# Turning the query weights on TensorE instead of by DMA, one slab fewer with normalized queries, and a new instruction order, in a four-layer attention and GLU kernel

## The chip, the cores and the metric

The kernel runs on one core of one Trainium2 chip. The metric is the device time of one execution in microseconds (us), and a kernel's time is the median of several executions. The core has five engines with an instruction queue each: TensorE (PE) for matrix products, VectorE (DVE), ScalarE (ACT), GpSimd (POOL) and SyncE (SP). SP here only issues DMA transfers, a transposing kind among them. Each engine executes its queue in order and waits on semaphores for the others.

## The reference

Four layers in a row act on x of 2048 positions by 512 channels, all in bf16: linear attention, GLU, linear attention, GLU. The weights are the same for both attentions and for both GLUs.

```
x = x + attention(layernorm(x));  x = x + glu(layernorm(x));  # twice

attention: q, k, v = x @ wqkv            # 32 heads of 16
  pq, pk = q @ w_phi, k @ w_phi          # per head, 16x16
  phi_q = [softmax(pq), softmax(-pq)];   phi_k likewise   # 32 features
  kv = phi_k^T v;   z = sum over positions of phi_k
  o = (phi_q kv) / (phi_q . z + 1e-6);   return o @ wo
glu: return (relu(x @ W_gate) * (x @ W_up)) @ W_down      # 1376 wide
```

## The kernel before

**Recording and order.** The kernel doesn't write its instruction streams out by hand. `build_kernel` records some 2100 operations with `op(...)`: an engine, a function that emits the instructions, the resources that it reads and writes, and an estimated cost. `schedule` then sorts them by a list scheduler with one priority for each operation, unpacked from the string `RANKS`; `MOVED` lists the operations (by number) which take their second engine (`alt`), mostly DVE in place of ACT or POOL and the other way round. `prepare` gives every operation the semaphore waits that its data and its buffers need. So `RANKS` and `MOVED` set the order on each engine, which engine some copies and small products use, and which of the buffers each tile takes. Once built, the order is fixed.

**Layers and tiles.** Layers are numbered 0 (attention), 1 (GLU), 2 (attention), 3 (GLU). A tile t is 128 positions (16 tiles), a slab s four tiles. The names used below are those of the operations, with the layer first: K0.4 is the key product of layer 0, tile 4.

**Start.** SP loads x in pieces, the key weights, the query weights (`wqn`, L561, one transfer into a part of the `Wd` buffer) and the value weights; POOL loads tiles 8 to 15 of x (L567) once tile 7 has landed. Forty small products (L571) warm PE up. The per-head matrix w_phi is multiplied into the weights: for that, the key weights are turned on PE (`turn`, L587: four 128x128 transposes per piece of 128 rows, "WkT") and copied out of PSUM by ACT and DVE (L477, L478). The products with the block-diagonal BD (L606) give Wkp and Wqp. The query weights are turned by four DMA transposes instead (L595, "WqT", flag `WQ_DMA`).

**Layer norm** (`ln`): statistics on DVE (L620, L621), ln and exp on ACT for the reciprocal root (L629, L631), y on DVE (L646) or POOL (L645). y is turned to yT by a DMA transpose (L660), or, for the tiles in `PE_Y`, on PE (L655) with a copy.

**Keys and values** (`kv_tile`, `features`): K (four matmuls of 512 columns, L682, for the first tile L686), two exps on ACT with signs +1 and -1 (L695), the sum over each head's 16 features (L703 on DVE, or a half sum on POOL, L700, and the rest on DVE, L701, for tiles in `POOL_Z`), the reciprocal as ln and exp on ACT (L717, L718) or on DVE (L720), and the norm, a product in place on DVE (L708). V is four matmuls (L739) and a copy. `kv_sums` then adds up keys times values over the tiles on PE (L786, "kv") and masks the sums into `kvs` on DVE (L809, L812) and, if any slab of the layer has normalized queries, also into `kvn` (L796, L799).

**Queries, two forms.** For a slab in the set `NQ`, `q_tile` makes normalized queries tile by tile just as keys are made, and two DMA transposes turn them (L767, "qT"). `attn_tile_n` then needs 8 products of 68 columns ("Rn", L901), a reciprocal on ACT (L906, L908) and two products on DVE (L913). For any other slab, `q_chunk` makes the exps already turned, without a sum: four times four matmuls of 512 columns (L754) and two exps each (L758). `attn_tile` then has 8 products of 144 columns ("R", L837) whose extra columns hold the sums, copies of them (L851), a chain of small operations for both signs' coefficients (p L858, den L860, ln and exp L862 and L863, coefficient L864), three products t on DVE (L874, L879) and their sum o (L883 on DVE, L884 on POOL). `finish_tile` turns o by DMA (L931) or on PE (L926), multiplies with wo (L936) and adds to x (L939).

**GLU**: gate and up products (L966), relu on ACT (L973), product on DVE (L974), a remainder of 96 columns ("rem", L994), and the down product ("d", L1020, L1022) with the sum into x on DVE (L1028).

The GLU weights are loaded by SP (L1052 to L1058) in the order of its queue; between them stand DMA transposes.

Of the kernel before, what the change touches and what calls it, by code (L numbers as in the profile page):

```python
# [421 lines left out]
def build_kernel(nc, A_x, A_wqkv, A_w_phi, A_wo, B_x, B_W_gate, B_W_up, B_W_down, out):  # L422
# [169 lines left out]
    if ("sp", "wqn") in LOADS or ("pool", "wqn") in LOADS:  # L592
        if WQ_DMA:
            for ic in range(4):
                op("sp", lambda e, ic=ic: e.dma_start_transpose(t_wq.ap()[:, :, ic * 128:(ic + 1) * 128], wqn[:, ic, :]), reads=[c_wqn, c_wd], writes=[c_wqT[ic]], dma="tr", nbytes=500, name="WqT",  # L595
                   after=chain["sp"][-1:])
# [511 lines left out]
ROUNDS = 8  # L1108

RANKS = (  # L1110
    '#{oD9YzH6+4hSI#fCnB3k_Q(E0SLqg`3C|BoCoIzT>ujZIS7FVEeH$<1OyETMF$)R%LhURjRvs?(g61d^aSe%b_W9pD+pTvjt5x>Y5-pb^#>;i=m+!%rT`ZJ',
# [3 lines left out]
    ')&|E0y#@^j<Ok{p2nRX_K?j`&AO_9`p$E_h)CbcC76`Qm;scEVp9kFsRs_8O%m)bp7zpD7+XSfwxd1>1BnRLJHV94!$p>-=7zaEDG6-o0jR$Q7oCb^r?gwrK',
    'l?7x6GzfkNBL`##wFa^W+XoK@76ASSY6c?++6SixpausA90zO#ng#I(x(4G0)(27s83>yOIR;7xl?F!!1P6)+mIliOOa^NPbOyx*L<Z6Y3J6sP+XmML@&!o-',
    'd<LEe$_D%e_y$)7DhH$n>;}XJMFs{2g9d#DR|l{MR0hNawg!U*8V4r^0|!|KXa|)C_Xha}Vg>F6F$O6Hdj^RHr3Oa_Ne7Dtg$D))IR}dep#}s7dIwzx$Om8r',
    'tOgMW_6L9kR0kIZbq7`lD+ZqgO9wCpEe09|6b3s6SO=;G<p**FxCS!@I0yU&@dbJY$^|F}>jYp1uLiXRng?G6JqGj!kp|cVNCtuj_5|4le+F9xss--`aR$By',
    'ItN1qE(bvc1qYi2Jq2+Ej|DIYvj><3vId3*-3E3B83uj@#s;1S;0A04F9uBpga<tb>;)(XP6o6GT?VKJzy|FGc?V(#6a_{FV+GO#st39U%LG~nr3EMi<_Aj!',
    'umwK_a0Y$`IRrxnHU{Vg`voBd<p#b5AP4USumlGM;s#{~(gREb(gxoHv<8?5g#)(-qzCi^Dg{aePz4?Z!vfj`#|6O!Km~6HZU*rNzz1pti3Pm{(*{ik%?BO_',  # L1120
    '?FY#Qfd#t-`UQ^!A_h7Ilm-6=X9l1Ls|QR6(*;=tiU-OBmj_b>y9a&*PzLk`X9dOu`2_+8*awCO^9C{o*anmbm;^Nit^<$<cLVkYD+lribp<2_j0ckhF$dQN',
    '!UyjM1O);Ft_DK~jRXk?a0HqLO$9Lp`Ul(x!v@C(3<uc;t_6GtGY6^z%?1AjH3nA%Ed=5PYX_MJUj()X(FSn`-38tTcn8r3@CQ%?9R}<J5C`Z6`v>3!hy~CF',
    'HU+c=8wP6y+y;{e;RLw{Mh89wf(2~`k_KV~69?Z00SAW$Ee9+IAqKMrHwHcivIUL>iv{ci9|tuDxCd_rTL&Qr*90X72L{vyLI-FB$Ob0|cm`(#DF=cE`vwID',
    'RRz`s$OJYA76&p1&IMHleFt0z69(-AX$Fl290unFUIpm|qXj+(od!P!@CJwn{smD5+yrI^tprO3QwE0x9tKJVI0n=MyalHPx&?OzF9qTRVFMlnIR)ee_XH3G',
    '4h0Yes|HgAXa)-gCI?{$TLzZ}&;=<4<^`q(vjh?bP6fmSs0HB#W(02qbq4PQp9V4n=md8K4FzNcWdv;ptOX7Rhz6nsQUtFA3j{a?MFoTfPX`PIfCdu<Wd%D0',
    'NCk@oBn9;a3I<9A2nPBD!UQJ;as~qh`~<-S>IJ6+ECyr*$OX0qQU(15odpmE<pr7qoC696_ysZrzXVSOqywo1umd^-Ed`7OHwCQ)vjZdqXa#u%GX%Q?tOO|p',
    '*98s-^Z|+jkOg-H^#sBN`2(K?N(09P$pn@JXafxdxB}S(X$98;`vaT=xdIvjzyi<%;{p=|vj8Fmu?3k0S_Ci!_yl?d@C0rI5(Mi8r~`Wh7zIQHX#}(cnF4_W',
    'F9bCN76Neu*aZRwOaxQ~vj&z0#scsIRRk^ufd&W#i3i{Wy#($AI|QHvE(JUUgaj)C5d{DQE(34}Nd-^`s|5@OBL<NL!3W|8S_bk45eS3^e+PpE6$t$XMFf}z',
    '_y<M?A_sj0_XWcT(g({14F=BzxCJW(zXgv56bCd1-UVU?y9Nsfd<7i`&jvIF76x1f+XX-dJO*I~2?Y-aRtBgBPX-kS0S0adSO)$B0R<lh$pxGRECp}{-2|cr',
    ')ds-^3I(G9qXvux5(TvcCI)#1wF43db_MDNqXVl1zXtOJw*zzppanh!)CRc*B?X=Z-~(X<%mr5ilmcA@MFTbi+XKi0wgTh>Yy+VLr30e`qy^go&jO<YqykX_',  # L1130
    'GX?zw0|wIrNC%JvyaW*j>jf191_ed~B?RXKas;&kD+E&mg#~y6wga02l>|crg#>W|o&x3rS_NAKSp<{=)dL#>-2<lrrUOm_=mO0I&I5A>AOoKR@&ZW%;{cii',
    'lmuG>69P~HI|C~MyaUbz%>&p1I{^s-!~&fIfdUr=F9YiW+5=DmR0GQckOEZ$-~vbjVF6DAAp!^i`2i0CJO!}?T?GpTBL%<(GzNbK)C7|SAO+e4a|F=@w*?~v',
    '{{$ul-UQ<XAq1}l7zTR<nFL$~76rHi4+R+o<OBc%h6C~hbOp=?`U7<Yp#}H?V+7L#=>(wzK?J!4sRR)O)dJiDxdW*I%mVxZC<Sx}{sbHaL<6P*$^x1KSOpvc',
    'V*}O#j05Qdzyuou#RCrmZ2|BFG6VVn2m>_&jRRl<hyxV_r2_Z><pYrf`2-dLg9E$*1_Vh2R|4V!djc*5QUi+ugaIA{`U2MhF$7Bls02p^bpp`?8w4-|9|SW4',
    '5(8QS0|Z_JKLf4;#sKF8e*_-|8wI)qrUjb>@dQ8w%mjx6hy-c`#stv?fdmN#>I60d;{??OHv{Yfh6G~<Rs$3S?gI}5h6UOIqy*&zq691i-UFfo^#QpA7z8u~',
    'Hw2XfjswpGDg$i-)&#5rz613GECa0vPy<*4B?mYIs{-%>CIm17dIaVI?gCE$a|5XZKLjHKEdzQ3A_8#(^a2F~=>bs$YXeII1qAT|a{*2S8U(@u76TRp_XG9<',
    '$pbh9Jp)Dpj{;`{vI4&WW&@uBuK}3@!~?hlyaC(=?F487CIf&1A_K7k&jZ2(*#eLQ&;k_!83Y{#U<4`z2Ll5GiUe!~f&{Sxv;(pPegoM9u?E%yz63r4^#=O{',
    'k_F!c*aNo&Zv;dHhXjBG%ma4<!2=frjs!^p>jOvxwgg@T2?O&3Mg*Y(cm%HlPXyEg3IqoP3<OmIzXJ^eW(Hsfm;-qP5d$9qU;)Jfk^vV3v;wRG9RxiD_5*JN',
    'rUZ%wZ3FQG1qGo1JOd>IZUP?zRs#3~y8`<Fd;?Sjj|1-mo&zcd{{sI5b_BlyGy`1$i2{KD7y>#1q5=g1djnqskph+jmjh7)asw3xYXl?$4g);`=>U@gF#|^e',
    'tpl(E-vaUjKmy4E-2n&$a{@vFWdel)cmfFo!~p^U<^VqeSpuB^X##lw9{_>^D*&YdhXI5DGy?Dek^?OOt^sfYNC8CwZ3G4a6az2>Vgs%OpaUEPy#jv&?g8xq',  # L1140
    'hXURK$O2&no&@s(?E)kN=mW+B5CM1r{{eyl!vrS;vI7SJO#vtas{;W8a0B@Q?*do^R|UHR*8}7Lz5<s7O#>YP_yJZ0LIt1!!vK>5cm?GG=>mKN(*lVEKm!2;',
    '3j<sPr~>5yLIeN;_W~XPTLYa0b^<8_Lj-*SssauKkpTz-kpnga+5!pzM+8~}w*mkKZvr0z!T>`7<p6^K2Lf9G0t1x-1OxL0ssw8S+yZ(6VFJJd&jF<bY6C?A',
    'fCJkB`vUy}Q~;6yX8;@lYXQLl>H-u3=K=%*W&(W!c>@{)b_1LNU;=^zK?4~BDgq(|SOSIuh5_9Gbpbm9x&!0^paNn6bOWXV1_N^d9s)T6egLHaE&|~LLjsrr',
    'hyvpQCjxl_sRDEYlL1QtzyUS^jRO1wWCKb9y#wL^o&g{P3j*-~e*&`t=Kz!ey8$%=0s@2rM*wyJg95Mt*a2k&%>g$8I0DoG;Q`+OQUS36F9DkYF#^K@JORM~',
    'IRl9SuL7?Cf&d`^ZvbThVgS|v@&Vca-~q7!7XlaqodLiA&H|4BWCDNzi~!RCc>$*Zs{yG14go{~(EzFd$p9w<@c}sj<N|L2J_6MN`~i~ybpwY0%K>lztO1q+',
    '1p%@Fq5&=eR06{TGXb;#iUFMhm;sdlkO9&HO#;OMS^?1lWB{!IDgiA4y#XcxcL8hx8382$n*-qhcK}=fg#a@EY5_n2#sMz^fdQ@nMgSB6ECJ8~1Od7L?*IV-',
    '>j94ei~=YD-T)>5I{=FT$N?$<&H#7-o&fd%ya0XyxdF@oGyx|7HvsnmqyVA-Kmg_e7XcaoY62htngAgIUIIb^Z~?ynBLRp2DFH|TJ^|POdjU@ZG66jS{{XE5',
    '@Bj@08v$1V3jy^4_5hLsFacizIss7uoB)sjWdK?LQUJIBasbN!7y(%T+yMpwUI0@800DIX8UYgkIRLN#_W-&99Rh6t9RvLVivtn@X#*1jQUcrnLIcMGz5(h1',
    '%>r@)69Mx9$^i-kECROxQv!|xM*+A2i2yAEg8>x<BmqnU-2!X^=K)*-T?1(W{sIsJX9DN}G6E$60|H$F;R5>sIs-8Q!T})z<^)IsSp&fWM*~R#3IewQ;sNLY',
    'RRE3wV*>gBr~#h=egaAXm;e<5i31D+jQ|+}%mEw&$^-oamH|NmssUmGmjQMGLI42*Cjo8&wgCPC*#Y1Hz5wn3wgLG7l>w9hp8!b!R{(th*#OP~W&xT3aRDX*',  # L1150
    'AOfKQ5CcB|4g&815d!o8g#kAKwE;~4gafSsasjIVSOGNwV*zdehyiW`(gD!{JObYVX8~RTbOBre)d0i*i~(T)djKl|5dl>JXaNiY#{hi*+W;Z~h5(8H(*QI8',
    'r~tYGXaJ`GdH@Rm0RWr=d;uN+?Equ}aR4|0GXh2d#{$X#kpNTyO98R~&j48gdI3HF$N)?MP6NpS4ge?umjamqK><$zwE&j@N&pf8)Bt<{K>&XNbN~$j6##q!',
    '>;cvRE&%)h0|ANyV*t$n8vrN(AOZCN3;}=u{Q$E8SOA#-DFE^SQ2?L-PyjCgivR)un*c-re*iH6>H{ePTm!oRmH@N>X#m#%9RQ;MFaXd1>i}i|Ujgg@^8h*k',
    'P5=@BKLOqX#Q<yoJpdd45dby-JOE4pjsQ3SBLZLmMF6Y-B>)fr%K{_-BLEEm1OQV2Rsc%?8311ZP60#$qyaJj2>=QJ0{}Gu1pxj41^^EM',
# [68 lines left out]
```

## Time and profile before

| | us |
|---|---|
| median of 5 runs | 385.37 (384.63 to 387.58) |
| profiled execution, time | 385.38 |
| its span | 383.6 |
| PE busy | 370.3 |
| DVE busy | 294.0 |
| ACT busy | 199.5 |
| POOL busy | 57.9 |

The span runs from the first to the last instruction of the profiled execution; its time has a little more at both ends. A line of the timeline or of the groups has the start and length in us, the engine, the line of the code, the operation, what it writes from what, and in brackets the engine's idle time before it and what ended that. "PEld" is the loading of weights into PE; "PEclk" or "granted clock" the share of full speed that PE was given. A matmul's record covers its whole way through the array, so that records of matmuls that follow each other overlap. In the chain of the work that ended last, each piece is charged only from the end of the piece before, so that a run of equal pieces there gives the pace at which they follow each other.

The chain's largest shares are the GLU's gate and up products (L966, 34%), the down products (L1020, 17%), wo (L936, 7%) and, of the other engines, DVE's norms (L708, 5%), ACT's exps of the features (L695, 5%) and DVE's sums (L703, 4%).

### The profile page before, as it was taken

The numbers are of one execution on the slowest core, as the hardware profiler recorded it, in microseconds if no ns is written. First come the engines' busy times: TensorE is split into PE (matmuls) and PEld (weight loads), VectorE is DVE, ScalarE is ACT, GpSimd is POOL, SyncE is SP. The second block draws the span as 40 slices with busy tenths as digits, with TensorE's granted clock in tenths as the row PEclk, the third lists the DMA queues.
The fourth block names the chain that finished last, engine by engine and source line by source line (L and its number), as shares of the span: only waits on it lengthen the run. The fifth ranks groups of instructions, "written<-read, shape, count | busy, mean of one in ns | idle before, by whom it ended". The sixth has DMA issues, their size and how long they took to land.

```text
span 383.6 us, 6614 instructions
## 1 busy us (share of the span) xinstructions
PE 370.3 (97%) x2413; PEld 205.2 (54%) x2455; DVE 294.0 (77%) x640; ACT 199.5 (52%) x615; POOL 57.9 (15%) x120
## 2 busy tenths in 40 slices
PE   8699999899999999999999999999999999999997
PEld 6344455677755544444444446577766454444443
DVE  7689998999779785564678999999879593633334
ACT  5689999654453422244218997873544433221300
POOL 1437520221021010000002011030022321000000
PEclk9899999999999999999999999999999999999999
DMA  7944798133522231310022200313613222101102
GB/s 230 198 81 85 141 304 183 38 61 65 82 56 42 41 44 38 59 29 14 15 41 41 43 1 7 65 29 57 100 38 70 55 43 55 24 20 41 43 0 82
DMA packets 71472, 25.52 MB, mean 67 GB/s; under 512 B 62640, under 2 KB 71184, under 8 KB 71440
## 3 DMA queue, kind: packets, MB, share of 16 engines
q1 hardware_dynamic: 68320, 21.97, 28.5%
q10 hardware_dynamic: 2832, 2.08, 1.7%
q0 software_dynamic: 288, 1.05, 1.0%
q8 instruction: 19, 0.31, 0.4%
q14 instruction: 13, 0.11, 0.1%
HBM read 8.44 MB, written 2.10 MB: 27 GB/s over the span
## 4 chain that ended last, share of the span: by engine, by line
PE 68%; DVE 17%; ACT 8%; DMA 4%; issue 1%; SPq 1%; POOL 0%; DVEq 0%
PE pb L966 34%; PE pb L1020 17%; PE pb L936 7%; DVE phik L708 5%; ACT phik L695 5%; DVE z L703 4%; PE pb L994 3%; PE pb L837 2%; DMA yT<-Wd 2%; PE pb L1022 2%; DMA Wd<-in_A_wqkv_dram 2%; DVE z L701 1%; PE pb L682 1%; PE pb L754 1%; DVE rz L720 1%
## 5 line engine op out<-in xcount | busy, mean ns | idle before, releaser
L973 ACT ACTIVATE gate<-pb 128x512 bf16<-128x512 f32 (+1 forms) x100 | 51.1, 512 | 78.6 <-PE pb L966 76.4
L974 DVE TENSOR_TENSOR expq<-gate,pb 128x512 bf16<-128x512 bf16 (+1 forms) x100 | 56.9, 575 | 39.1 <-PE pb L966 35.2
L966 PE MATMUL pb<-yT,Wu 128*128 128x512 bf16 (+1 forms) x395 | 83.2, 336 | 0.3
L966 PE MATMUL pb<-yT,Wg 128*128 128x512 bf16 (+1 forms) x395 | 81.7, 336 | 0.3
L1020 PE MATMUL pb<-Wd,expq 128*128 128x512 bf16 (+2 forms) x315 | 74.2, 372 | 0.6
L966 PEld LDWEIGHTS pb<-yT,Wu 128*128 128x128 bf16 x400 | 38.7, 98 | 29.0
L966 PEld LDWEIGHTS pb<-yT,Wg 128*128 128x128 bf16 x400 | 38.6, 98 | 28.7 <-ACT yT L477 0.3
L1020 PEld LDWEIGHTS pb<-Wd,expq 128*128 128x128 bf16 x330 | 31.6, 98 | 35.8 <-ACT gate L973 0.3
L695 ACT ACTIVATE phik<-pb 128x512 bf16<-128x512 f32 x80 | 45.2, 675 | 7.9 <-PE pb L682 7.8
L620 DVE BATCH_NORM_STATS2 stats<-x_sb 128x6 f32<-128x512 bf16 x64 | 43.0, 684 | 0.6
L1028 DVE TENSOR_TENSOR x_sb<-x_sb,pb 128x512 bf16<-128x512 bf16 (+2 forms) x33 | 22.1, 668 | 19.9 <-PE pb L1022 19.6
L629 ACT ACTIVATE lnv<-mv,eps 128x1 f32<-128x1 f32 (+1 forms) x58 | 16.5, 292 | 35.5 <-DVE mv L621 35.3
L700 POOL TENSOR_TENSOR t<-phik 128x512 f32<-128x512 bf16 x16 | 20.1, 1262 | 92.3 <-ACT phik L695 84.0
L936 PE MATMUL pb<-wo,oT 128*128 128x512 bf16 x124 | 31.8, 379 | 1.1 <-DMA oT<-o 0.9
L682 PE MATMUL pb<-Wkp,yT 128*128 128x512 bf16 x123 | 31.0, 393 | 0.8 <-ACT yT L477 0.8
L646 DVE TENSOR_SCALAR y<-x_sb,mv,rstd 128x512 bf16<-128x512 bf16 x63 | 25.7, 423 | 7.3 <-ACT rstd L631 7.0
L739 PE MATMUL pb<-wv,yT 128*128 128x512 bf16 x124 | 29.9, 379 | 0.2
L703 DVE TENSOR_REDUCE z<-phik 128x64 f32<-128x1024 bf16 x24 | 28.4, 1198 | 0.1
L758 ACT ACTIVATE expq<-pb 128x512 bf16<-128x512 f32 x48 | 27.2, 639 | 2.3 <-PE pb L754 2.3
L708 DVE TENSOR_TENSOR phik<-phik,rz 128x1024 bf16<-128x1024 bf16 x40 | 26.6, 701 | 0.1
L874 DVE TENSOR_TENSOR t<-pb,sm 128x384 bf16<-128x384 f32 x48 | 25.2, 547 | 0.7 <-POOL sm L864 0.5
L939 DVE TENSOR_TENSOR x_sb<-x_sb,pb 128x512 bf16<-128x512 bf16 x32 | 21.7, 679 | 4.1 <-PE pb L936 4.1
(92 smaller groups left out, 403.7 us busy)
## 6 DMA issues: line engine op xcount, KB each, us to landing
out_dram<-x_sb ACTq DMA_DIRECT2D x15, 128.0 KB, 1.7
Wg<-in_B_W_gate_dram SPq DMA_DIRECT2D x2, 640.0 KB, 7.0
Wu<-in_B_W_up_dram SPq DMA_DIRECT2D x2, 640.0 KB, 8.2
Wd<-in_B_W_down_dram SPq DMA_DIRECT2D x1, 1280.0 KB, 7.2
x_sb<-in_A_x_dram POOLq DMA_DIRECT2D x2, 512.0 KB, 7.0
yT<-y SPq DMA_TRANSPOSE x55, 2.5
Wd<-in_A_wqkv_dram SPq DMA_DIRECT2D x2, 256.0 KB, 2.9
Wd<-in_A_wqkv_dram SPq DMA_DIRECT2D x1, 512.0 KB, 6.7
```

The source lines that it names most:

```text
L620: op("dve", lambda e, t=t: e.bn_stats(stats[:, t, :], x_sb[:, t, :]), reads=[res("x", t)], writes=[res("st", t)], ii=600, lat=690, name=f" ...
L682: i = e.matmul(kt.ap(), src.ap()[:, ic, c0:c0 + 128], W[:, ic, :], start=(ic == 0), stop=(ic == 3))
L695: op("act", lambda e, s=s: e.activation(ft.ap()[:, :, s, :], kt.ap().rearrange("p (g f) -> p g f", f=64), ACT.Exp, scale=(1.0, -1.0)[s]), ...
L703: op("dve", lambda e: e.tensor_reduce(zt.ap()[:, zo].rearrange("p (a b) -> p a b", b=2), flat().rearrange("p (a f b) -> p a b f", f=16, b= ...
L708: op("dve", lambda e: e.tensor_tensor(flat().rearrange("p (a f b) -> p a f b", f=16, b=2), flat().rearrange("p (a f b) -> p a f b", f=16, ...
L739: i = e.matmul(vt.ap(), src.ap()[:, ic, c0:c0 + 128], wv[:, ic, :], start=(ic == 0), stop=(ic == 3))
L758: op("act", lambda e, g=g: e.activation(es[g][0].ap(), qt.ap(), ACT.Exp, scale=(1.0, -1.0)[g]), reads=[qr], writes=[es[g][1]], ii=477, lat ...
L936: i = e.matmul(wt.ap(), oT_.ap()[:, c, :], wo[:, c, :], start=(c == 0), stop=(c == 3))
L966: i = e.matmul(pt.ap()[:, 0:n], W[:, ic, fc * 128:(fc + 1) * 128], src.ap()[:, ic, a * 128:b * 128], start=(ic == 0), stop=(ic == 3))
L973: op("act", lambda e: e.activation(st_.ap()[:, 0:n], gt.ap()[:, 0:n], ACT.Relu), reads=[gr], writes=[sr], ii=110 + n * .72, lat=230 + n * ...
L974: op("dve", lambda e: e.tensor_tensor(ht.ap()[:, a * 128:b * 128], st_.ap()[:, 0:n], ut.ap()[:, 0:n], ALU.mult), reads=[sr, ur], writes=[h ...
L1020: i = e.matmul(pt.ap()[:, 0:n1 - n0], hT[l, s, fc].ap()[:, c:c + 128], Wd[:, fc, n0:n1], start=(fc == 0), stop=False)
```

## The change

Three settings change, and with the last of them the whole order:

- `WQ_DMA` is off. The query weights are turned as the key weights are: 16 PE transposes (L587) into PSUM and four copies (two of them on ACT, two on DVE) in place of four DMA transposes. (The diff also changes what the DMA transposes would wait for; with the flag off, that line isn't executed.)
- `NQ` loses (0, 0). Slab 0 of layer 0 takes `q_chunk` and `attn_tile`; the masks into `kvn` in layer 0 fall away. Slab 0 of layer 2 keeps its normalized queries.
- `RANKS` and `MOVED` are others, since there are other operations. As built, PE has in the opening K0.0 (three of its four matmuls), WqT, K0.0, WqT, WqT, the turn of y of tile 1, WqT, Wqp, the turns of y of tiles 3 and 2, Wqp, K0.1, K0.3, V0.3, V0.2, V0.0, K0.2, V0.1, Wqp, V0.4, Wqp, K0.4, K0.6 and then the other keys and values; all query chunks of layer 0 come behind V0.15. Before, it had K0.0, K0.1, a Wqp product, V0.0, K0.2, Wqp, K0.3, Wqp, V0.3, V0.1, Wqp, V0.2, three query tiles, K0.5, and query chunks between keys and values. K2.2 and V2.2, which stood inside the GLU of layer 1, stand behind it. SP loads wo and all GLU weights directly behind the last yT of layer 0. Three value copies of layer 0 are on DVE in place of one.

```diff
-                   after=chain["sp"][-1:])
+                   after=chain["sp"][-1:] + chain["pool"][-1:])
         else:
             turn(lambda ic: wqn[:, ic, :], lambda ic: [c_wqn, c_wd], t_wq, c_wqT, "WqT", ["act", "dve", "act", "dve"])
...
 RANKS = (
-    '#{oD9YzH6+4hSI#fCnB3k_Q(E0SLqg`3C|BoCoIzT>ujZIS7FVEeH$<1OyETMF$)R%LhURjRvs?(g61d^aSe%b_W9pD+pTvjt5x>Y5-pb^#>;i=m+!%rT`ZJ',
...
+    '9sqX)M*%<xF9<gXe*!)T-Uk8*!T_EG5eDW1I|w}pRs}x@*9O=J`~-LhNe46t1PB8NDhRIwB?t-#D+i(m$p;Sr$_HEr0ssL3Q3n733;;X`I|dE_0|2cB9S9!?',
...
 MOVED = (
-    75, 139, 271, 497, 563, 588, 595, 612, 619, 659, 663, 684, 715, 735, 756, 759, 779, 783, 787, 1462, 1471, 1480, 1528, 1553, 1560, 1600, 1601,
-    1648, 1652, 1676, 1680, 1700, 1704, 1728, 1744, 1752, 1768, 1772, 1776, 1800,
+    73, 75, 93, 101, 143, 245, 305, 325, 471, 472, 475, 481, 497, 547, 599, 627, 643, 644, 647, 651, 667, 692, 699, 715, 716, 740, 767, 771, 788, 791,
+    812, 1470, 1488, 1536, 1544, 1561, 1568, 1592, 1612, 1640, 1656, 1657, 1680, 1681, 1688, 1705, 1712, 1729, 1732, 1736, 1752, 1760, 1780, 1800,
 )
...
-WQ_DMA = True
+WQ_DMA = False
...
-NQ = {(2, 0), (0, 0)}
+NQ = {(2, 0)}
```

More of the change, by code (lines that the diff above doesn't have):

```diff
@@ L1110 @@
 RANKS = (
-    '#{oD9YzH6+4hSI#fCnB3k_Q(E0SLqg`3C|BoCoIzT>ujZIS7FVEeH$<1OyETMF$)R%LhURjRvs?(g61d^aSe%b_W9pD+pTvjt5x>Y5-pb^#>;i=m+!%rT`ZJ',
-    '-vvVe>Hrh~C<uE8A^>v-YXBt(QwPQe;Ri1W-Uk=}1PG!B000jF!v*sP=?AU{H3%~Z{|Chf3;-7g2ml=jCJ2-U2M7=d{0FxNa|H+p-v=ZJF$gyY)dwyJ1qgQs',
-    '&j%U?*$0jWFb6~jA_%7gkp~Y5j|asBn+GfaUI(lP><0n{tp*ebQ3j9(uLp+*00_zlHwXs+DhSR8{szqkk_0RWO$1U01_<W{g9qjYr3X<5zXzrVRso|2Uk3mN',
-    '8VIKbmj-GF{RasMW(5ET)da!@;RZnlmIprvV+St>3kc%}eFen^UIv8*+6K@B8wlhEDG2%oI|pY68wU~yOa;CNnFj3z83!K-=?3lwsRz6Vy$6#9We4^Jum-#a',
@@ L1115 @@
[L1115 to L1154, printed above, removed]
+    '9sqX)M*%<xF9<gXe*!)T-Uk8*!T_EG5eDW1I|w}pRs}x@*9O=J`~-LhNe46t1PB8NDhRIwB?t-#D+i(m$p;Sr$_HEr0ssL3Q3n733;;X`I|dE_0|2cB9S9!?',
@@ new lines @@
+    '7623g1ppTa1OSQ#90(Br3IMhRBM77bD+VM8%>|+X6#yIr2mqG_r3YFD4FD4W69|C^e+OIw2>>AoY5?g55eO{^4hUla1_9v%1^^}q5&+c%6bL>CTmUl&3jnbP',
+    '8VDi?3<#eGga=s$c>#z9;0Im?3kZ=1!~tdi76?rT^aVZ!IS4HSK?M~E5(w)D^anu*ya750L<a~6@dNS)HV7~X#Rs_uRR?te2LKreum|S{qzCQ?dk41%H3#Vj',
+    'A_Wf!vIpA-#|9z?p$0ApLI+a^DhJO8^9P0pm<I_6)CV94tq0Nv2ME0e`Ub)W1_=5GCkLAc&<9ip9taZ$kO#d7MF+D7{Ri9z1_#Cml?Q4ET?eKId<Sp`Xa)oa',
+    'x(CAs7zecm5(kb4@dkYd8V7s^<p%%<+y@{B&IZ2*uLnE@;RoFZ1_kB>UI(rRP6F=(F$muWWC!9083$DbwgPGfX9xBNTLxeT)dwsH*9Gqe=mo?FZU@u`ZwEIA',
@@ new lines @@
+    '^#*VTF$ehu5CAm>8UQ&5z6PfUSqG~IT?PRL{st%q<OGHWHwCr_pazl#%?2d~U<c0w?geHCD+v1qV+XDVjt1uj?*$$QO9%S~2?rMk8wZmH9|zC{GY9bnH3<I(',
+    '*apl8G6<grqy|R@K?igOhX-Z`7X~;7BL|`fTL+#7>jtj|s0Tj>S_hd1$p-WWxCS-{atDA1P6q=AiwCC$wg$omQU{I&yasg!-UeR>CI^uQf(P~m<Ofj(xdw#>',
+    '%?BL^VF!-}NCyK3rUvl`od=2sGzTvS(+B7Vng&1z>IPW_+XfW}mIn|Ai3f`YL<Xz}!3MVmb_Wp$YX*!5o(Ba66bGCI$_9i6(FWuOAqU<C(guYGKn17<#0HN9',
+    '`~`ak8wP&{ng<O8>IJL?{RWW*vIY_cQw5a<N(b5ofdxGVJO+9OB?n&yMFtNAqXlvWj|Wc&*#m$C<^}`=^#|<+PX_!3p$FIl{RBJ&kpTz-f&{$-s{_;n+XHR|',
@@ new lines @@
+    'tpsfav<6`YivzI%;|Ie7Uj@Ge-vc`Wa|OExTn5<(MhEx?zz2*3$Oh;K@CR21bO#6qa|Y%IzXt#adIdcNBL+AK!3QY_@&+gf{0Bn@_XpVqDF!VEss%#@{|B50',
+    'm<4MGg9n!eVg_Xd3j(SF90#oiCIuS^*aSxhPzUb^@dN<~5C!lBg#~y8d<16%Xa#x)Z3evr?E~utaRyxl;|6C2$po1NB?bEj)doxltN<qnItQf&aR=H5G6(Dj',
+    'qX(%61qg`-k_U|issySA%mzdS3I}KhkOmkC)(7|pxCi+M%Lo1k?FXv|&IhmtHwF+04G6;rc?MPoJO`ZyP6Z1FYzF-UPzI9+I|pnB-v-DB_695mn+6RAz6S>f',
+    '4F_Qa&IF(ba|8wk@&(ofy9Uz*1qXEpeg^>ut_9Ht;RXx_5(WMR_Xa2iX$O=C2nP%Ymk0R;CI<fn+67kxsRn!nF$D_+LkAuPas)63_5>XURRl~1%LWAnQ3bRI',
@@ new lines @@
+    'hzE@a*9QUycLm%9)dkE1Z3is|-35UI5d|0q#|Hog@CG^ta|iAQeFiZGsRWG%6b8ly&<3Cd8U>*RN(EyD*#tTRW(1Z6+Xd$Z2L{*$wFhqo?gVEAR0e|vp9LBQ',
+    'HU?M+!v!P;-UN~bFa@s#SO(4oegqr^umrmW83qmpvjpY^4+ixGCj}J-zXgy5hy{BEhXttxG6uW_F$84>s|6tiYXs~BV+5N8QU$;U#Rbs?j0PqIlLYq!KL*VN',
+    '<pjb7hX#xVQv|vNw*_Mc9|oiZP6R3jZU$flUIlOk7X?WLxCH0~WCcY8@B^X*Zv+4ZWd~dZNd!Ixx&(Lx9tBth_XDW{IRj<|6a<zAtpno)N(RydAqEWveFTsM',
+    'lm^QM2?cisGX*OJ4+p&kIt9Q5MFWNf-vz@2B?P<#1O?Ou69lXTQUn<Vas%!I&jiW@)&%ebbOizjRtDt;5Ck0s!UVDfSp+WyY6N8kvjN-$wgf5!eg((`=mHu9',
@@ new lines @@
+    'iUcDBVFgwMxdk}{;01vMTLdfwg9BOwPz09*LIxxS9|AH3%L6L}Tm)$ZrvyR-0|l4{vj(69?Ezi{5(FX!-2_(!s07;tN(3wh3<Z@1{RM&s(giRENCr6uY6Zy!',
+    'F9z%e?FF0$&jzdpyaz`Gcm@^+ss}v>3I=utc?T{Ax(4?J>Id@$1O|ZyQwEs_I0h#MMFmL)(+1rJ4hIVd$OWDSrUgL;Pz6W@#{@11<puZ!l?0Ooq6K6I(*!dH',
+    'P6kT`HUxwO`UMsS!37%yKn5HJT?8!!lm+4imIF)$qXrNL8UxG)vjxQlDFv_vng#y^I|R!FwFR98IR*Oz69v}<gavj5#{;tiLjr6AGXy^aa{~zkYXkZMxdX-o',
+    'bpwI}RRbOaUjt(U+yYz!>;(x1j|Hs)H3ilNBnKb_>I0tx{{v(L6$G#XbOXo&ZUU|YQU=`vI|FV6DFhb-`~xflxdKK7WCWZ8E&~??9Rzs=g9J?kq65wYy8|}^',
@@ new lines @@
+    'Z3I{ZD+4nFssWe-G6A~)xC6BUlL3eVHUgXi9|27T1q8|iz6In3O9f2^djvHEpaXvcQUfXjO#|HmPy-SJsRJAXbOM$F(f}3%6a{tydjiD(qy@wUeg=XCPX#mu',
+    'm;_=4GzRGe3I*8(iUk7%jRcDYI|Z}^TLp3kfCkhA69%ybYXy1)e*}XCLIrsQBm|`e?F2>!rUWPjfCYaA^91h%uLN)e$_3{H2nFi|b_ARRE(9n9^#sKPJp*t9',
+    '=>?|+k^_DN(F17%0t5vE<N}HVg91wg>jU5fF9g~Go&);=kON)=nFBrpQv>V+00Zm-T?1JI1_Uq!_5=9@AO$!CR|eq(=mU8J*8?~MNdx@?%>p3<Bm;{Cg#_dS',
+    '4+J9vZv(CbngsF!)&q?L9|QFQPXm+#AOi*i?E;bnQ3QPju>_d}i3Onq;0Cw_KLvCI2L*8j&jkkrR0Z<}u?A@dbp@ye3j|sP^aJ|@76jo19|evCRR-Gvxdh_`',
@@ new lines @@
+    'w*<xo!2}Eh;s$60s{|he#R3im-vkx~_yi{e5d_r(Ed<~Lh69NMz5-|iG6YHk3IoytM*~y>O9ABq5CfY8;{(kDbp+l6Oa!h1Z3CzSrUQ%v`~tuOcLPHM*8(L2',
+    '!~*yO+5@`;0t1=@{sXrHK?4~Bw*v?RvICO?S_4@E3<C`VNCO@O;saL$#RED7d;|IeR0CTB?gH-tq5@$9LIdXl;R0X-Yz34AP6KHLG6T#5n**N&ECsX$#|4%I',
+    'AO_F`)&j%?hy=O=cmqcS0tNI0qXbU`0R+<m2?PEFi3EoPAp{!)L<EZh&jKn1z68tyU<7dlA_PVRJ_Nu7vIO}983Yal(gWoKqXRz#+ymzWl>?OmKm$Aj*a9L0',
+    'gaTUv1Ow{=;sWyn(*r{U7zBm{X9IWwH3N|Y>H@z4lL8n64g(znu>(c}Jp{Z1E(O8^zXM+cL<0*0y#mGp`UF4%CIjFB8Ul<0{{kig$OE+lv;*J*Vgzmj$pR4r',
@@ new lines @@
+    'O9M6o!veMgHU-K8Gz6Ce!2;?8)dIu=7zNG(kp!y(x&qMzBL&_8;sm__y8<)<4gr|}Isg{{o&gyEApoQSdI5m|6ajYudIFsR0|Ivkd;!V;Dgn&^Py+Y>uL95m',
+    '=>rM`2n1#Wk^(>kdjSCjZ34gn@&o_`z5`SQhy!m00|SBr8~_6W_5fA`odkpcgaMrc;{Xi;fdU=^umhz8JpoJuz5yu*Vh3pf@B&8wNCFuFK>|nw_yTeQ;{x*n',
+    '?*fSe8vrB##sdTb7y#`6Z~^ZCLIDQ?wFImKp#vZQY6IQ^fB{_sI0Z=oH3C)udjtLfhXZT`p#mNO;{hlE=>ib}G6FdQD*|2uI0B~w#sKgE(E{!OGy@m`d;+}z',
+    't^pweCjof^u>vpxYXIi~Q3I<1Q38zt76H@(AOUFtL;>yrfC32ug#vK^eFD`0g#)w#j|15Psss4~Y65oxiUKhMO#+qyD*;#l$N(t;Pyx3AR{~!EWdZ^LUjn5A',
@@ new lines @@
+    '&;X7D%>my6gabDO@&oAs4g%x>LIM{8b_1^fqysPm6a#AlRs!V!fCE+mj{@2RC<2rMaRbW&W&$Sz@d4%nEdufZHv(D!J^|4Hp8}fz;sL?}69V}GQv$dGVFH^1',
+    'xB&nHmjVX^&jGOj6ao_iyaE;i*a1uerveuN$pD%GS^~KN{{j920s`v+{Q;i=YyvX?JOEMvumRrzaRMCzY5}hS&H--#A_8Lpn*s9xvI2|%`T=MF^Z}p&>;a|$',
+    'rT_{7dIL=WZvuJ%DFQ44&;tAb^8vL1_yKzW3jvA%4*}!=(g7v`#{n<_5CYKwNC5@{MgV^SYXLg|OaWd13<C85g#k+fhXOAHKLSAkR{>K2f&n)G$^k(Dm;!zR',
+    'F#$gT2LWIKZ2^M;kpR~LRRIM8SOPZzWdZa8=m5h2#{wt-Q~^2xPXRyyGXZ@8jsd9vN&z7OoB<~Qask!=qXN$WF9B}>lmK7=QvfLdSpXUVtpO?kqXD!5Jp!iy',
@@ new lines @@
+    'tN|MXDFed+mH<)#r2*9e906MaVF6|V4FPom^Z-f#wgHC$0Re6R@Bl~vE&)yewgB+}HUXRfmjGt~Yyf@%KmbDkzyOE<m;lEBWdJPzVE`onX98ma!2>=53Id7&',
+    '`v9{7@d82s<^e$jWdi{N9{{WZqyiNMQUZ<wjRG|Q5CK&Jzye<ZN&-&;VgmO9R{%2tM*_(ME&?S2BLY|hi2)G;kOHOxMFJH9+yO-ZIsz&J4+Gi(VgO(Q^#kew',
+    'AOcAOkpeLSeFNwLJOV8N83OwOodVMVq5#wZ`~kuNh5-@+Z~|}uh5(2G7y^p{cmcWrXaY|F-2uh{y8){JX#gk#&;cX@Cj$2Yp#iu6h630Ck^tZUo&XX7{Q!6X',
+    'jsWEWVguU&sR5M%-T*`b90GF!LjgYkr2_T=nE`GAlmXcRi2&IEngUn>`T(Z^T>(u2a{(&=XaSi5_5v>g6$4}faRF=r0RqVZMFC;~H39bkP65*Z4+81{umDB@',
@@ L1155 @@
+    'v;YVJxd4X%Gy$#vmjROivH(N?bOBxgBmuVoI{{q)b^*)*wE&C(asVs=O8}?>;Q{La+yFQMkO7?l1OdMRo&q!gfdT&jz5r1HfB+o<A^~&&bpV(Fr~obiG5}ct',
+    'r2wq}qX60f>;RAeBLUU{paS^-WC7OzTmg#!PyjvvTL3Wt)BwK#OaK)D9RS||jR1oHg#fw$H~`B4IRKRaBLFr4vj8RlZ2(jN+W?>d%K_&AB?0~b$N@$IvH=?c',
+    'k^u|>p#a4J;Q&zpe*l62j{z(IX93~>!2$IE%m6$AS^=5>!2o^$@&LR5!~g&R=>VSqssITAr~!5WRRD7U69MJ`-2gcONdSBRcK~Dn8v%I$JpeBN&H#@9A^-&e',
+    'eE={3',
 )
 MOVED = (
-    75, 139, 271, 497, 563, 588, 595, 612, 619, 659, 663, 684, 715, 735, 756, 759, 779, 783, 787, 1462, 1471, 1480, 1528, 1553, 1560, 1600, 1601,
```

## The prediction

> **What bounds the kernel now.** First the page's busy line and the table of three stretches: the GLU of layer 1 (from its first gate matmul at 72.24 to the first layer-2 query tile at 200.63), the kernel behind it, and inside that the 38 us of layer 2's features.
>
> ```profile
> PE 370.3 (97%) x2413; PEld 205.2 (54%) x2455; DVE 294.0 (77%) x640; ACT 199.5 (52%) x615; POOL 57.9 (15%) x120
> 72.24:200.63 128.39, 127.65 (x758) 71.37 (x770) 98.05 (x223) 49.91 (x171) 11.75 (x27) 1.00 0.24 45
> 203.70:242.00 38.30, 38.10 (x301) 19.60 (x302) 37.81 (x58) 35.80 (x94) 3.98 (x4) 1.00 0.13 25
> ```
>
> Columns: stretch, its length, then PE, PEld, DVE, ACT and POOL busy, granted clock, DMA. A 97% PE is not yet a PE at its rate: its records overlap. So I count matmuls at the pace they have back to back in the chain (512 columns x4 in 0.86 us; 65 columns 0.034; 144 columns 0.062; 128 columns about 0.06). That content is 128.3 us in 72.24 to 200.63, which lasts 128.39: no slack. From 200.63 to the first layer-3 gate matmul (253.22) it is 52.4 of 52.6 us. From there to the end it is 126.6 of 130.4, with 2.4 us of tail behind the last matmul. Before 72.24 it is only 58.7. Of 383.6 us some 13.5 are slack, and nearly all of it lies before the first GLU. There the timeline and a fine table show where it goes.
>
> ```profile
> 9.87 6.45 SPq L595 DMA_TRANSPOSE yT<-Wd  x4
> 14.74 0.40 PE L606 MATMUL pb<-BD,yT 128*128 128x128 bf16 x4 [2.10 <-DMA yT<-Wd]
> 15.83 1.80 PE L682 MATMUL pb<-Wkp,yT 128*128 128x512 bf16 x4
> 17.86 1.77 PE L682 MATMUL pb<-Wkp,yT 128*128 128x512 bf16 x4
> 20.23 0.40 PE L606 MATMUL pb<-BD,yT 128*128 128x128 bf16 x4 [0.60 <-DMA yT<-Wd]
> 26.30 3.62 PE L682 MATMUL pb<-Wkp,yT 128*128 128x512 bf16 x16
> ```
>
> The fine table, columns as above:
>
> ```profile
> 13.00:14.00 1.00, 0.00 (x0) 0.00 (x0) 1.00 (x3) 1.00 (x3) 0.37 (x2) 1.00 1.31 71
> 17.00:18.00 1.00, 1.00 (x7) 0.72 (x6) 0.00 (x0) 0.33 (x1) 0.00 (x0) 0.50 2.01 273
> ```
>
> PE stands in order behind a Wqp product that waits for a DMA-turned query weight; then it runs one window at half clock: four 512-column matmuls take 1.80 us where 0.86 is usual. Meanwhile DVE and ACT starve (0.00 and 0.33 in 17 to 18). Tile 4 and later begin only at 26.30. The chain carries the same, and then two engines in turn:
>
> ```profile
> 3.16 6.69 DMA Wd<-in_A_wqkv_dram
> 12.50 7.68 DMA yT<-Wd
> 36.31 2.92 ACT phik L695 x6
> 53.09 4.22 DVE phik L708 x7
> 57.31 1.13 DVE z L703
> ```
>
> From 24.8 to about 51 ACT is full (an exp every 0.487 us), after it DVE (a norm every 0.603, a full sum 1.13).
>
> **The change, part by part.** *Query weights on PE.* Out go four DMA transposes (6.45 us of SP's queue, four landings of 4.8 to 7.7 us). In come 16 PE transposes and four copies. The same work on the key weights (L587) takes 16 in 1.57 us; I take 1.5 on PE, and 0.34 each for two DVE copies (row 419 ns, less overlap) and 0.49 each for two on ACT. The Trainium skill speaks against this twice. "VectorE: DVE Perf Modes", section "The three transpose paths", has 390 ns for one 128x128 on TensorE, hence 6.2 us for 16. The row decides: 1.5. "TensorE: Matmul & The Clock Gate", Part 4, says that transposes do not count as busy for the clock. The new list has little else between 9.1 and 12.5, so by the page the next window of 3.4 us would run at half clock and cost 1.7 us. The granted clock here fell at 15.94 and returned at 19.36, so windows of that length end at 12.53 and 15.94. The window before 12.53 held 0.86 us of plain matmuls and 0.72 of transposes and kept the clock; the one before 15.94 held 1.2 us of plain ones and lost it. Counted with transposes that is orderly (1.58 kept, 1.2 lost); without, it is not. I take no loss; by the page it would be 1.7 us, of which a wait below hides 1.5.
>
> *Slab 0 of layer 0 without normalized queries.* On DVE out: 4 x (1.13 + 0.60) for sum and norm, 2 x 0.42 for kvn, 8 x 0.33 for the outputs (L913), 10.4 us. In: twelve t (8 x 0.46, 4 x 0.33), four sums o at 0.33, five small ones of 0.12, 6.9 us; with the two copies above 0.7. Two casts of weights go to ACT (-1.2), one BD comes from POOL (+0.2), and two more value copies come from ACT (+1.2). DVE in all -2.6 us up to the second layer-1 y, but -5.5 up to the kvs masks and +2.9 behind them. ACT: 8 x 0.15 for ln and exp of z out, lden from 12 steps to 8, 12 sm copies in: within 0.6 us of now. PE: 32 products of 144 columns for 32 of 68, +1.0 us. SP loses eight qT transposes, the first two of which stood for 4.6 us and the next four for 8.2 ahead of the Wd load; all GLU weights now come before the masks. Nothing of layer 0 waits for Wd, so that is worth 0.
>
> *The order: the opening.* The list is walked with the durations above.
> - The query weights land at 9.85 as now. K0.0's fourth matmul stands behind the first turn: K0.0 ends at 10.5, its exps start 1.6 us later than now (8.97).
> - ACT then has no gap: two exps, three yT copies, a Wqp copy, exp of K0.1 until 14.8.
> - POOL sums K0.1 (1.16), two nmr, y0.4 (0.76) done at 17.4, now 19.7. SP has nothing ahead of it; landing 2.5 us later, 19.9. PE has by then done K and V of tiles 0 to 3 (18.5) and waits 1.4 us; then V0.4, Wqp, K0.4 until 21.9.
> - DVE: the sum of tile 0 at 11.7, four stats, then stats of tile 11, whose load lands now at 18.2 (11.5 + 6.7); without the turns beside it I take 17.5. Behind it 3.1 us of list, y0.6 at 20.6, landed at 23.3.
>
> K0.6 thus starts at 23.3. From there to the first GLU matmul PE has 42 groups of four (11 K, 11 V, 16 Q, 4 wo) x 0.864 = 36.3, key-value sums 4.4, R of six tiles 3.0, transposes 1.0: 44.7 us. Now the same stretch from 26.30 has 43.0 us of work and takes 45.9, 2.9 lost. I take 2.0 lost: norms end near 48.5, ahead of PE's sums (52), but the masks are followed by a longer chain (sm, p, den, ln, exp, coefficient, t, o), of 4 us against 2.6 now, which ten query chunks cover for the most part. 23.3 + 44.7 + 2.0 = 70.0, against 72.24: **-2.2 us**. PE alone would allow 68.0; the losses of now, 70.9.
>
> *The order: the rest.* Layer 1's GLU holds the same PE work less K2.2 and V2.2 (1.73 us), which move into layer 2's stage. There DVE was full: up to the second y of layer 3 its list grows by 2.6 us (Z 1.13, norm 0.60, two y and small ones), PE's to 54.1. At the bound the two cancel within -0.4 to +0.9; I take 0. The last GLU has the same PE list; 1.4 us of stall at its start may go or double: 0, ends -1.4 and +1.4.
>
> Sum: 383.6 - 2.2 = 381.4 span. The profiled execution took 385.38, 1.78 more than its span, and that is the median of the runs (385.37) too. **383.2 us.**
>
> **The rivals.** *A, the gain is given back.* What opens early ends at the same time, since ACT, full from 24.8 on, has no less to do (for: its row of exps; against: its list up to the last yT copy sums to 56 us, and with some 7 us idle in the opening ends at 63, 7 us before it is needed), or the attention chain after the masks costs 2 us more than assumed. 385.4 (384 to 386.5).
>
> *B, slower: the new first transposes meet the loads.* yT0.4 and yT0.6 are issued at 17 to 21, while tiles 8 to 15 still arrive; the query weights' turns took 4.8 to 7.7 us in such company, not 2.5. At 7.7, V0.4 starts at 25.1, PE idles 6 us, loses its clock for a window (8 matmuls, 1.7 us), and K0.6 starts near 28.5: 28.5 + 44.7 + 2.0 = 75.2, +3.0, **388.4**. It decides once K0.6 comes after 25.5. Against: the DMA share is down to 0.05 in 20 to 21.
>
> *C, layer 2's stage takes DVE's extra 2.6 us and the GLU before it does not shorten,* because a wait fills the 1.73. 385.8 to 386.8.
>
> *D, nothing much of it shows,* as all turns were hidden: excluded by the 2.10 us wait and the half clock.
>
> **How the numbers follow.** Main case 0.50 (own range 381.0 to 384.6: K0.6 at 22 to 24, losses 1.5 to 2.5), A 0.23, B 0.15, C 0.10, D 0.02. What a measurement can tell from no change is 0.5%, 1.9 us: under 383.4 faster, over 387.3 slower. Main gives 0.40 faster and 0.10 same; A 0.02, 0.20 and 0.01; B 0.15 slower; C 0.01, 0.03 and 0.06, with some of the last two cases together; D same. Together 0.43, 0.35 and 0.22. The range takes main's lower end, a little more for the 1.4 us, and most of B: 380.5 to 388.0.
>
> **What would show it.** No wait on the turned weights and a clock of 1.00 from 9 to 20 in the fine table; K0.6 near 23 and the first gate matmul near 70 in the timeline; 126.6 us from there to layer 2's first query tile, then 54 to the next first gate matmul. Wrong it is if yT0.4 lands after 22, if the clock falls, if PE waits between the masks and the first wo for over 3 us, or if the GLU stretches hold waits of more than 1 us.

## The result, and where the time went

The changed kernel takes 384.78 us (median of 44 runs, 383.69 to 386.76) against 385.6 us for the kernel before beside it (79 runs): a ratio of 0.9973, with a 95% interval of 0.9963 to 0.9983. That is 0.27% faster, about 1 us (the medians differ by 0.8), where 2.2 us (0.56%) had been forecast. The span of its profiled execution is 383.3 us, before 383.6.

The page of the changed kernel, its busy line:

```profile
PE 370.6 (97%) x2429; PEld 205.8 (54%) x2471; DVE 292.2 (76%) x646; ACT 199.8 (52%) x618; POOL 58.3 (15%) x123
```

Three stretches of the changed kernel (first gate matmul to first layer-2 query tile, from there to the first layer-3 gate matmul, from there to the end) and two microseconds of its opening; the columns are stretch, length, then PE, PEld, DVE, ACT and POOL busy, granted clock, DMA share, GB/s:

```profile
68.63:196.64 128.01, 126.27 (x751) 70.34 (x764) 94.14 (x219) 47.82 (x165) 10.34 (x22) 1.00 0.21 40
196.64:252.83 56.19, 53.56 (x404) 27.54 (x410) 55.02 (x98) 49.66 (x138) 5.38 (x7) 1.00 0.21 41
252.83:383.30 130.47, 127.44 (x766) 71.80 (x778) 81.04 (x178) 42.07 (x138) 15.52 (x29) 1.00 0.23 47
13.00:14.00 1.00, 1.00 (x6) 0.49 (x5) 1.00 (x2) 1.00 (x5) 0.06 (x1) 1.00 0.91 242
17.00:18.00 1.00, 1.00 (x7) 0.39 (x4) 1.00 (x3) 1.00 (x3) 1.00 (x4) 1.00 0.00 0
```

Cut at the same four marks, by the start of the matmul record (so the marks of before lie 0.2 us earlier than in the prediction, which had them from the chain, where a piece starts only at the end of the one before):

| stretch | before | after | difference | forecast |
|---|---|---|---|---|
| start to first gate matmul | 72.08 | 68.63 | -3.45 | -2.2 |
| GLU of layer 1 | 128.39 | 128.01 | -0.38 | -1.73 |
| layer-2 stage | 52.59 | 56.19 | +3.60 | +1.73 |
| last GLU and tail | 130.52 | 130.51 | -0.01 | 0 |

The opening brought more than forecast. PE, ACT and DVE are full in both microseconds in which they had starved before, and the clock stays at 1.00. Then 1.35 us and 1.87 us more than forecast were spent in the two middle stretches. Two waits of PE account for most of both. The chain of the changed kernel, start and length of each piece:

```profile
78.73 0.86 PE pb L936 x4
79.60 1.05 issue
80.65 0.82 PE pb L994 x8
...
206.75 0.32 DVE y L646
207.08 0.60 DVE phik L708
207.68 0.52 DVE z L703
208.19 4.20 DMA yT<-y
212.39 0.05 issue
212.44 1.05 PE pb L739 x4
```

PE's timeline for the same two places, with the idle time and its releaser in brackets:

```profile
80.65 0.82 PE L994 MATMUL pb<-Wr,yT 128*128 128x192 bf16 x8 [1.05 <-issue]
212.44 3.63 PE L739 MATMUL pb<-wv,yT 128*128 128x512 bf16 x15 [1.39 <-DMA yT<-y]
```

The first wait is that of rem1.0.1, the remainder product of tiles 2 and 3 of layer 1's first slab, which needs their turned y. The profile puts its wait down to nothing ("issue"). The landing times of the two transposes, issued from 74.63 on (the second near 75.94), point at the second of them:

```profile
DMA to landing us min/median/max: 2.5/3.6/4.6
```

With 4.6 us it lands near 80.5, which is when PE goes on. In the trace of before both of the same pair land in 2.5, and rem1.0.1 does not wait. The DMA view of before for that pair (count, median us from issue to landing):

```profile
yT<-y SPq DMA_TRANSPOSE x2, 2.5
```

The second wait is that of V2.13, the value product of tile 13. Its y comes on DVE only at 206.68, behind sums and norms of the full layer-2 stage; its transpose is issued on SP behind two query transposes at 208.19 and takes 4.20 us to land. With 2.5 us it would have landed at 210.7, ahead of PE's 211.05.

### The profile page after: what moved, and what is told of

The parts are those of the page before. It is cut to its first block, busy times and chain, and to the rows that moved or that the text cites. A ratio compares the mean times of both kernels' runs of the same rounds, so it can differ in the third digit from the quotient of the medians.

```text
span 383.3 us, 6646 instructions
## 1 busy us (share of the span) xinstructions
PE 370.6 (97%) x2429; PEld 205.8 (54%) x2471; DVE 292.2 (76%) x646; ACT 199.8 (52%) x618; POOL 58.3 (15%) x123
## 4 chain that ended last, share of the span: by engine, by line
PE 77%; DVE 10%; ACT 5%; DMA 5%; issue 2%; POOL 1%; SPq 1%
PE pb L966 36%; PE pb L1020 18%; PE pb L936 7%; PE pb L754 4%; PE pb L837 3%; PE pb L994 3%; DVE z L701 2%; DVE phik L708 2%; PE pb L1022 2%; PE pb L786 2%; DMA yT<-y 2%; DMA Wd<-in_A_wqkv_dram 2%; ACT phik L695 2%; DVE z L703 1%; ACT vaug L477 1%
## 5 line engine op out<-in xcount | busy, mean ns | idle before, releaser
L974 DVE TENSOR_TENSOR expq<-gate,pb 128x512 bf16<-128x512 bf16 (+1 forms) x100 | 57.0, 575 | 46.7 <-PE pb L966 46.3
L966 PE MATMUL pb<-yT,Wu 128*128 128x512 bf16 (+1 forms) x396 | 82.8, 336 | 0.3
L966 PE MATMUL pb<-yT,Wg 128*128 128x512 bf16 (+1 forms) x393 | 81.3, 336 | 0.4
L1020 PE MATMUL pb<-Wd,expq 128*128 128x512 bf16 (+2 forms) x320 | 75.4, 372 | 0.5
L966 PEld LDWEIGHTS pb<-yT,Wg 128*128 128x128 bf16 x400 | 38.4, 98 | 30.1 <-DMA yT<-y 0.4
L966 PEld LDWEIGHTS pb<-yT,Wu 128*128 128x128 bf16 x400 | 38.9, 98 | 28.8
L695 ACT ACTIVATE phik<-pb 128x512 bf16<-128x512 f32 x72 | 39.8, 644 | 2.1 <-PE pb L682 1.0
L700 POOL TENSOR_TENSOR t<-phik 128x512 f32<-128x512 bf16 x16 | 19.1, 1196 | 88.4 <-ACT phik L695 83.2
L758 ACT ACTIVATE expq<-pb 128x512 bf16<-128x512 f32 x56 | 30.7, 603 | 3.1 <-PE pb L754 2.9
L936 PE MATMUL pb<-wo,oT 128*128 128x512 bf16 x120 | 30.9, 379 | 0.5
L874 DVE TENSOR_TENSOR t<-pb,sm 128x384 bf16<-128x384 f32 x56 | 29.4, 547 | 1.5 <-POOL sm L864 1.5
L682 PE MATMUL pb<-Wkp,yT 128*128 128x512 bf16 x124 | 29.5, 379 | 0.2
L646 DVE TENSOR_SCALAR y<-x_sb,mv,rstd 128x512 bf16<-128x512 bf16 x63 | 27.3, 441 | 2.5 <-ACT rstd L631 2.0
L851 ACT ACTIVATE sm<-pb 128x48 f32<-128x48 f32 (+1 forms) x84 | 14.5, 211 | 26.5 <-PE pb L837 26.4
L754 PE MATMUL pb<-yT,Wqp 128*128 128x512 bf16 x106 | 25.9, 379 | 0.5
```

What stands on the lines that cost most here:

```text
L682: i = e.matmul(kt.ap(), src.ap()[:, ic, c0:c0 + 128], W[:, ic, :], start=(ic == 0), stop=(ic == 3))
L695: op("act", lambda e, s=s: e.activation(ft.ap()[:, :, s, :], kt.ap().rearrange("p (g f) -> p g f", f=64), ACT.Exp, scale=(1.0, -1.0)[s]), ...
L754: i = e.matmul(qt.ap(), Wqp[:, ic, c * 128:(c + 1) * 128], src.ap()[:, ic, :], start=(ic == 0), stop=(ic == 3))
L758: op("act", lambda e, g=g: e.activation(es[g][0].ap(), qt.ap(), ACT.Exp, scale=(1.0, -1.0)[g]), reads=[qr], writes=[es[g][1]], ii=477, lat ...
L874: return e.tensor_tensor(tt_.ap()[:, b, 0:384].rearrange("p (c h d) -> p c h d", h=8, d=16), pt.ap()[:, 0:432].rearrange("p (c w) -> p c w ...
L936: i = e.matmul(wt.ap(), oT_.ap()[:, c, :], wo[:, c, :], start=(c == 0), stop=(c == 3))
```

## The experiments

In all four kernels the order is a fixed list for each engine, so that single operations can be moved without moving others; it shifts the line numbers behind it by 4 (L966 is L970):

```diff
+        queue = {e: sorted((o for o in ops if o.eng == e), key=lambda o: o.prio) for e in ENGINES}
...
                 for o in ready[e]:
+                    if o is not queue[e][-1]:
+                        continue
...
             ready[e].remove(o)
+            queue[e].pop()
```

`RANKS` then holds places in these lists. The kernel before ran beside the four 32 times, median 385.30 us. The ratios, with their intervals, are taken over all runs and are not quite the quotients of the medians.

**1. New opening, old order behind it.**

```diff
 settings of the changed kernel (WQ_DMA off, NQ without (0, 0))
 each engine up to the first gate matmul: order of the changed kernel
-each engine behind it: order of the changed kernel
+each engine behind it: order of the kernel before
```

> The changed kernel's settings and its order on every engine up to the first gate matmul; every operation behind that in the order of the kernel before (K2.2 and V2.2 again inside the GLU of layer 1). Theory T (the new opening is worth 3.4 us, and the new order behind it gives them back by waits of its own and by work put into the full layer-2 stage): first gate matmul near 68.6, then 311.5 us as in the kernel before, span 380.1 to 380.7, 3 us or 0.8% under the kernel before. Rival R (the middle ends when it ends, whatever the order, because DVE and ACT have no less to do): span 383.0 to 383.8, ratio 0.998 to 1.001.

Measured: 385.81 us, ratio 1.0007 (0.9985 to 1.0028), span 383.7. The first gate matmul comes at 68.91, as early as hoped, and nothing of it is left at the end. PE's and ACT's timeline of this kernel:

```profile
71.24 0.29 ACT L633 ACTIVATE lnv<-mv,eps 128x1 f32<-128x1 f32 x1 [2.02 <-DVE mv L625]
72.61 0.61 PE L970 MATMUL pb<-yT,Wg 128*128 128x256 bf16 x4 [1.68 <-ACT gate L977]
273.03 1.25 PE L1024 MATMUL pb<-Wd,expq 128*128 128x512 bf16 x5 [0.92 <-DMA expq<-hr]
```

The join itself made the first wait: the old order has the norm of tile 2 on ACT ahead of the first relu, and here tile 2's statistics are later than PE, so ACT stands 2.02 us and PE runs out of banks. 0.92 us more go to a transpose of the remainder in the last GLU, which landed in 4.2 us where it took 2.4 before. The stretches are 130.35, 52.72 and 131.72. By number this is rival R's result, but two waits in two places make up 2.6 of the 3.28 us that it takes longer than before behind the first gate matmul, one of them of the join's making. It shows that the opening's gain is not kept by an order that was laid out for another opening; it doesn't show that no order keeps it.

**2. Old opening, new order behind it.**

```diff
 settings of the kernel before (WQ_DMA on, NQ with (0, 0))
 each engine up to the first gate matmul: order of the kernel before
-each engine behind it: order of the kernel before
+each engine behind it: order of the changed kernel
```

> The mirror image: the kernel before, with its own settings and its own order up to the first gate matmul; every operation behind that in the changed kernel's order. T: first gate matmul at 72.1, then 314.7 us as in the changed kernel, span 386.3 to 387.0, ratio 1.007 to 1.009. R: span near 383.6, ratio within 0.2% of 1.

Measured: 386.38 us, ratio 1.0021 (0.9994 to 1.0048), span 386.9. T's 1.007 to 1.009 is missed; R's 0.2% lies within the interval. Stretches and PE's timeline of this kernel:

```profile
73.58:201.71 128.13, 127.42 (x763) 70.52 (x762) 93.84 (x217) 47.10 (x164) 10.31 (x22) 1.00 0.20 40
201.71:256.31 54.60, 53.85 (x411) 27.59 (x410) 53.95 (x98) 49.52 (x138) 5.36 (x7) 1.00 0.23 42
```

```profile
85.81 0.82 PE L998 MATMUL pb<-Wr,yT 128*128 128x192 bf16 x8 [0.52 <-issue]
```

Behind the gate matmul it takes 313.3 us, 1.8 more than before and not T's 3.2: rem1.0.1 waits again, for 0.52 this time, and V2.13 not at all, although y and its transpose come at the same distance from the first query tile as in the changed kernel. Here that transpose was not late. So the order doesn't make these waits by itself; it leaves no margin for a transpose that lands 1.7 to 2.1 us later than usual, and which transposes do so differs between kernels that have the same order there. (The first gate matmul is late in this profiled execution, 73.58 against 72.08 with the same order, because PE ran at half clock once more, from 70.9 to 74.3; by an estimate, half of 73.58 to 74.33, that adds 0.4 us behind the gate matmul.)

**3. The turn alone.**

```diff
-WQ_DMA = True
+WQ_DMA = False
 (order of the kernel before; WqT on PE around K0.0's last matmul and yT0.1,
  copies on DVE behind y0.1 and y0.3, on ACT behind yT0.3)
```

> The kernel before with the query weights turned on TensorE (16 transposes behind K0.0, copies two on DVE and two on ACT) and nothing else changed: normalized queries and order as before. T: the wait of 2.10 us and the half-clock window go, the loads of x land at 4 to 5 us instead of 7; first gate matmul 1.5 to 3 us earlier than 72.1 and as much at the end, ratio 0.992 to 0.996. Rival (the opening's gain comes from the new order and the missing normalized queries of layer 0, since PE's old order still has all its work behind tile 4): under 1 us, ratio 0.998 to 1.000.

Measured: 386.18 us, ratio 1.0008 (0.9987 to 1.0030), span 384.4: no gain. PE's timeline of this kernel:

```profile
22.42 2.75 PE L686 MATMUL pb<-Wqp,yT 128*128 128x512 bf16 x12 [1.33 <-DVE mv L625]
66.22 0.30 PE L905 MATMUL pb<-kvn,expq 128*128 128x68 bf16 x4 [0.74 <-DMA expq<-phik]
82.58 0.82 PE L998 MATMUL pb<-Wr,yT 128*128 128x192 bf16 x8 [0.49 <-DMA yT<-y]
273.85 1.25 PE L1024 MATMUL pb<-Wd,expq 128*128 128x512 bf16 x5 [0.49 <-DMA expq<-hr]
```

The wait for the turned weights and the half-clock window are gone (granted clock 1.00 in all of the opening), the loads of tiles 8 to 15 land in 4.07 and 5.15 us, and the keys behind tile 4 start at 25.0 instead of 26.3. At the first gate matmul 0.72 of these 1.3 us are left (71.36), at the end nothing: a query transpose, a y transpose and a remainder transpose come late to products that did not wait for them before, although every engine's order behind the first gate matmul is that of the kernel before. For the same wait of rem1.0.1 the profile names the y transpose here (its pair landed in 4.1 and 4.9 us). So the rival is right on this point: the opening's 3.45 us are not the turn's alone. Whether they come from the missing normalized queries (10.4 us of DVE work out, 6.9 in) or from the order was not tried apart; nor was the turn put back to DMA inside the new order.

The 32 runs of the kernel before say nearly the same without any edit. In 22 of them the mean granted clock was 0.991 to 0.996, which is one or two half-clock windows as in its profile; in 10 it was 1.000. The medians are 385.27 and 385.39: in most executions of the old order the half clock costs nothing at the end. But the slow tail goes with it: all nine executions over 385.81 (385.96 to 388.43) are among the 22, and the mean of the 22 lies 0.67 us above that of the ten.

**4. The changed kernel with its two waits taken out.**

```diff
 DVE: ... y2.10
+y2.13
 Zh2.1 Z2.2 norm2.0 Z2.1
-y2.13
 SP:  ... yT2.10
+yT2.13
 qT2.0.1 qT2.0.0
-yT2.13
 PE:  ... wo0.5
-rem1.0.1
 u1.0.5.0 d1.1.0
+rem1.0.1
```

> The changed kernel with two moves: y of layer 2, tile 13 comes on DVE right behind that of tile 10 and its transpose on SP ahead of the two query transposes (V2.13 waits 1.39 us for it), and the second half of the remainder of slab 0 (rem1.0.1, waits 1.05 us) comes on PE 1.5 us of work later, behind the down product of tile 1. T: both waits go and are not replaced, span 1.8 to 2.4 us under 383.3, ratio to the kernel before 0.991 to 0.993. Rival R: the time turns up in other waits of the same stages, span 382.8 or more.

Measured: 382.84 us (9 runs), ratio 0.9928 (0.9903 to 0.9954), which is below the changed kernel's interval. Theory T's number. Its first two stretches:

```profile
71.22:197.99 126.77, 126.77 (x763) 70.36 (x763) 93.89 (x219) 47.65 (x165) 10.29 (x22) 1.00 0.21 40
197.99:252.60 54.61, 53.86 (x412) 27.60 (x411) 53.98 (x98) 49.55 (x138) 5.38 (x7) 1.00 0.23 42
```

They are 1.24 and 1.58 us shorter than the changed kernel's, no new wait has come in either, and PE's busy time fills the first to the last hundredth. The pair of y transposes for rem1.0.1 is as late as ever (landing times in this kernel):

```profile
DMA to landing us min/median/max: 2.5/3.5/4.4
```

Only nobody waits for it now. That is what the two moves bought: margin. The profiled execution ended at 383.1 all the same, because its opening was late by 2.6 us (below); the median span of the nine runs is 381.0, the changed kernel's 382.95. This version is faster than both kernels: by 0.72% than the kernel before (by the medians 0.64%), and by about 0.45% (0.9928 over 0.9973) than the changed one. The waits are not those of one profiled execution: all 44 runs of the changed kernel (383.69 or more) took longer than each of the eight runs of this version at full clock (383.34 at most). Each move alone was not run, so what each of the two is worth stays open; the 1.94 us between the medians is somewhat less than the 2.44 that both waits took in the one profile.

## Why the prediction was right and wrong

- **The opening's walk: right up to one landing.** K0.0 ended at 10.35 (forecast 10.5), the exps of K0.1 at 14.6 (14.8), y of tile 4 at 17.2 (17.4), its transpose landed at 19.8 (19.9). From K0.6 to the first gate matmul it took 46.8 us (44.7 + 2.0 = 46.7). What was mis-sized is the load of tiles 8 to 11: it was taken to land at 17.5 and landed at 15.4, 4.1 us after its issue, where it had taken 6.7 beside the DMA transposes. So y0.6 was not late, and K0.6 came at 21.8 instead of 23.3. That accounts for the 1.25 us by which -3.45 beats -2.2.
- **The slack of the kernel before: a slip.** The 13.5 us are those of the opening alone (72.24 less 58.7); with the 3.8 of the last stretch (130.4 less 126.6) it is over 17. No other term was worked out from it.
- **Transposes and the clock: right.** By the Trainium skill ("TensorE: Matmul & The Clock Gate", Part 4) they should not have counted; in the changed kernel the clock stays at 1.00 behind the stretch with the 16 new transposes. Run 4 shows it more sharply (below).
- **The turn as the source of the gain: wrong as a reason.** The prediction took the 2.10 us wait and the half-clock window to lie on the path to the end. Run 3 took both away, had its first gate matmul 0.72 us earlier and ended no earlier.
- **"The order: the rest": the step that failed.** It added up PE's and DVE's lists, found that the two middle stretches cancel within -0.4 to +0.9, and took 0. Measured on the same marks they add 3.22 us, and two waits for late transposes make 2.44 of them; with these out (run 4) the stretches are 2.82 us shorter. The lists were added up rightly: with the two waits out, run 4 has 126.8 and 54.6 where 126.6 and 54.1 to 54.3 were forecast. What the sum could not see is when each transpose is issued and how late it may land. The walk through DMA landings, which met the opening within 0.2 us up to that one load, was not made behind the first gate matmul.
- **The rivals.** A (gain given back) has the nearest number, 385.4, but neither of its places: ACT and the chain behind the masks cost no more than assumed. C (a wait fills the 1.73 us in the GLU) named one of the two places; its other half, layer 2's stage bound by DVE's extra 2.6 us, fell with run 4: with more DVE work than before (53.98 us against 49.67), that stage took PE's 54.1 us and half a microsecond. B did not occur; the first two transposes landed in 2.5 us.
- The last GLU: forecast 0, measured -0.01.

## What to carry to other kernels

When PE is the bound, a sum of the engines' lists gives what an order can reach, not what it will take: for every operand that comes by DMA, compare the issue time plus a late landing with the time at which the consumer is due, and move the producer forward, or the consumer back, where the margin is under about 2 us, the delay of the late transposes here. A stall in the opening counts only if what follows it up to the next full stretch has no slack of its own; look first whether executions with and without the stall end at different times, in their slow tail as well as in the median. An order is not a sum of parts: in run 1, half of one joined to half of another made a wait at the join and had another one far behind it.
